# Bias rows, staircase rows and buffers of an attention and MLP kernel moved in its first stage

## The chip, the cores and the metric

One NeuronCore of a Trainium2 chip runs the whole program. The metric is device time in microseconds (us), the median over several executions. The kernel before has a median of 371.52 us in 11 runs (368.65 to 373.35). One further execution was profiled; it took 371.14 us, of which 369.4 us are its span, from the first to the last recorded instruction, and 1.74 us lie around it.

The core has five instruction queues. PE (TensorE) multiplies matrices, ACT (ScalarE) applies functions, DVE (VectorE) works on elements, POOL (GpSimd) does slower element work here and issues DMAs, and SP (SyncE) only issues DMAs. Every queue is worked off in order. PEld in the profile is the load of a stationary operand for PE.

## The reference

Eight batches of eight heads, 576 positions, head size 64, causal attention with an extra bias made of a cumulative sum, then a two-layer MLP whose activation is a hard swish:

```python
scores = scale * np.matmul(q, k.transpose(0, 1, 3, 2))
s_pos = np.maximum(s, 0.0)
cum = np.cumsum(s_pos, axis=-1)
bias = -(cum[:, :, :, None] - cum[:, :, None, :])
scores = np.where(causal, -1000000000.0, scores + np.minimum(bias, 0.0))
...
attn = attn / (np.sum(attn, axis=-1, keepdims=True) + 1e-09)
out = np.matmul(attn, v)
...
h = x @ w_in
g = h * np.clip(h + 3.0, 0.0, 6.0) / 6.0
return (g @ w_out).astype(np.float32)
```

x has 4608 rows (batch times position) and 512 columns (head times head size); w_in is 512 by 2048.

## The kernel before, in words

**Pairs.** The 64 heads are taken two at a time: 32 pairs p, four pairs (PPB) to a batch. The loop over p at L576 does the attention of a pair, and from p = 4 on it weaves in groups of the MLP (`group()`, L478: `m1` is the first layer, `m2` the second), as the batches become complete. The order of instructions on each engine is the order of the program text; no scheduler changes it.

**One q and k tile per pair.** A pair lives in one of NQK = 3 tiles `qks[p % 3]` (L84). Partitions 0 to 63 hold q and k transposed. Partitions 64 to 67 hold four bias rows, so that one matmul over 68 partitions adds the bias; `load_aug` (L135) copies them there out of `aug`, with one DMA for each head of the pair, 9 KB each. Partitions 68 to 127 hold a staircase, a constant pattern that makes masked entries of a diagonal block large and negative when the matmul runs over all 128 partitions. The staircase is used by pairs 4 and up; the first four pairs add a mask with a matmul of their own (`add_mask`, L273) and read 68 partitions only. `set_stair` (L506) writes it, two copies over partitions 64 to 127, so bias rows must be loaded after it. Before the change all three tiles get their staircase before the loop: tile 0 on DVE, tile 1 on ACT, tile 2 on DVE.

**The way of q, k and v.** SP loads q and k of a pair into `raws` (`load_qk`, L106) and v into `vraws` (`load_v`, L122). POOL casts q and k to 16 bits (`cast_qk`, L183) and v (`cast_v`, L198). PE transposes q and k (`transpose`, L217) and ACT and DVE copy the result into `qks`. In the loop, `get(i)` (L594) is the transpose for pair p+1, `scores(p, hh, g)` (L282) one of three parts of the scores of head hh with its exponential on ACT, `corner` (L317) the last 64 positions of both heads, `av` (L343) the product with v, `norm` (L373) the division on DVE. `scores` and `corner` of a pair wait for its bias rows.

**Who issues what.** On SP, after the first loads, the order is: bias rows of pair 0 (L561), q, k of pair 2, v of pair 1, q, k of pair 3, v of pair 2 (L562 to L567); then in iteration p: bias rows of pair p+2 (L579, for p below 4), q and k of pair p+4, v of pair p+3. On POOL: bias rows of pair 1 (L570), casts of v 0, q and k 1, v 1; then in iteration p: bias rows of p+2 (from p = 4), cast of q and k of p+2, cast of v of p+1, and one piece of the MLP weights (`next_weights`, L163: w_in in two pieces, w_out in four), a DMA that also casts to 16 bits.

**Semaphores of SP's DMAs.** SP's and ACT's DMAs go round eight semaphores; a DMA waits until the eighth before it has landed. So SP has at most eight transfers under way.

**Masks.** For pairs 4 and up, DVE takes the minimum of the exponentials and a mask (`masks_sb`, 128x640, L313 and L337).

Of the kernel before, what the change touches and what calls it, by code (L numbers as in the profile page):

```python
# [9 lines left out]
F32 = mybir.dt.float32  # L10
F16 = mybir.dt.float16
# [7 lines left out]
def kernel(  # L19
# [10 lines left out]
    nc = tc.nc  # L30
# [9 lines left out]
    NKC = DM // 128  # L40
    NFT = DFF // 128
    NBLK = NT // 512
    SPAD = 768
    NPE = 2 * PPB + 1
    NQK = 3
    NRAW = 3
    VW = 66

# [2 lines left out]

    jj, ii = np.arange(128)[:, None], np.arange(128)[None, :]
    tri = np.where(jj <= ii, 65504.0, 0.0)
    tri4 = np.where((jj <= ii) & (jj < 64), 65504.0, 0.0)[:, 0:64]
    masks_dram = nc.inline_tensor(
        np.concatenate([tri] * 4 + [tri4] * 2, axis=1).astype(np.float16), name="masks"
    )
    grp = (np.arange(128) * 61 // 128)[None, :]
    steps_r = np.arange(1, 61)[:, None]
    stair = np.zeros((128, 2, 128), np.float32)  # L60
# [13 lines left out]
    def keep(name, shape, dt, n=1):  # L74
        made = [
            cpool.tile(shape, dt, name=f"{name}{i}", tag=f"{name}{i}") for i in range(n)
        ]
        return made if n > 1 else made[0]
# [10 lines left out]
    w_in_sb = keep("w_in_sb", [128, NKC, DFF // 2], F16, 2)  # L89
    w_out_sb = keep("w_out_sb", [128, 4, DM], F16, 4)  # L90
    ident = keep("ident", [128, 128], F16)
    masks = keep("masks_sb", [128, 640], F16)
    neg_sb = keep("neg_sb", [128, 128], F16)
    stair_sb = keep("stair_sb", [128, 2, 128], F16)
    bias3 = keep("bias3", [128, 1], F32)
# [149 lines left out]
    def spread(p, i):  # L245
        jt, qk = J[p], qks[p % NQK]
        for par, n in ((0, 3), (1, 2)):
            c = 9 * i + par
            r, sl = 64 * (c % 2), c // 2
            src = jt[r : r + 64, sl : sl + n, :]  # L250
            ap = [list(x) for x in src.ap]
            ap.insert(1, [256, 2])
            nc.vector.tensor_copy(  # L253
                out=qk[0:64, :, i, 128 * par : 128 * par + 256 * n].rearrange(
                    "p h (s two c) -> p h s two c", two=2, c=128
                )[:, :, :, 0, :],
                in_=bass.AP(src.tensor, src.offset, ap),
            )

# [22 lines left out]
    def scores(p, hh, g):  # L282
        qT, kT = qk_of(p, hh)
        pt = Pof(p, hh)
        S = s_bank([128, 512], "S")
        masked = p < PPB
        if g == 0:
            if masked:
                add_mask(S, 128, 4)
            for j in range(4):  # L290
                c = slice(128 * j, 128 * (j + 1))
                mm(  # L292
                    S[:, c],
                    lhsT=kT[0:68, c] if masked else kT[:, c],
                    rhs=qT[0:68, c] if masked else qT[:, c],
                    start=(j == 0 and not masked),
                    stop=(j == 3),
                )
        else:
            for j in ((0, 3) if g == 1 else (1, 2)):  # L300
                c = OFF[j] - 512 * g
                w = 448 - 128 * j
                mm(  # L303
                    S[:, c : c + w],
                    lhsT=kT[0:68, 128 * j : 128 * (j + 1)],
                    rhs=qT[0:68, 128 * (j + 1) : SEQ],
                    start=(c == 0),
                    stop=(c != 0),
                )
        c = slice(512 * g, 512 * (g + 1))  # L310
        nc.scalar.activation(out=pt[:, c], in_=S, func=AF.Exp, scale=0.125)  # L311
        if g == 0 and not masked:
            nc.vector.tensor_tensor(  # L313
                out=pt[:, c], in0=pt[:, c], in1=masks[:, c], op=ALU.min
            )

    def corner(p):  # L317
        S = s_bank([128, 2, 64], "Sc")
        masked = p < PPB
        if masked:  # L320
            add_mask(S, 64, 2)
        for hh in range(2):
            qT, kT = qk_of(p, hh)
            r = 68 if masked else 128
            mm(  # L325
                S[:, hh, :],
                lhsT=kT[0:r, 512:640],
                rhs=qT[0:r, 512:576],
                start=(hh == 0 and not masked),
                stop=(hh == 1),  # L330
            )
        pc = PCs[p % 2][:, 0:128]
        nc.scalar.activation(
            out=pc, in_=S.rearrange("p h c -> p (h c)"), func=AF.Exp, scale=0.125
        )
        if not masked:
            nc.vector.tensor_tensor(out=pc, in0=pc, in1=masks[:, 512:640], op=ALU.min)  # L337

# [152 lines left out]

    s_all = work.tile([NHEADS, SEQ], F32, tag="s_all", bufs=1)
    nc.sync.dma_start(out=s_all, in_=s.rearrange("b h t -> (b h) t"))
    nc.scalar.dma_start(out=stair_sb, in_=stair_dram.ap())
    nc.scalar.dma_start(out=ident, in_=ident_dram.ap())
    load_qk(0, 0, nc.sync)
    load_qk(0, 1, nc.scalar)
    nc.scalar.dma_start(out=masks, in_=masks_dram.ap())  # L500
    nc.scalar.preload_act_table_set("natural_log_exp_and_others")
    load_v(0, nc.sync)
    for i in range(2):
        load_qk(1, i, nc.sync)

    def set_stair(i, copy):  # L506
        for hh in range(2):
# [8 lines left out]
    fill(nc.gpsimd, aug[:, 1:4, 0, :], 1.0)  # L516
    for i in range(NQK):
        init_va(i, nc.gpsimd)
    ones = work.tile([NHEADS, SEQ], F32, tag="ones", bufs=1)
    nc.vector.memset(ones, 1.0)  # L520
    nc.vector.memset(bias3, 3.0)
    for i in range(NQK):
        for hh in range(2):
            r = SEQ + 64 * hh
            nc.vector.memset(qks[i][0:64, hh, :, r : r + 64], 0.0)
    for t in Ps:
        fill(nc.vector, t[:, 1536:1664], 1.0)
    for t in PCs:
        fill(nc.vector, t[:, 128:192], 1.0)
    set_stair(0, nc.vector.tensor_copy)  # L530
    set_stair(1, nc.scalar.copy)


    idle = psum.tile([128, 512], F32, tag="s", bufs=2, name="idle")
    for i in range(44):
# [7 lines left out]
    )  # L543
    c8 = work.tile([NHEADS, SEQ], F32, tag="c8", bufs=1)
    nc.vector.tensor_tensor_scan(
        out=c8, data0=ones, data1=spos, initial=0.0, op0=ALU.mult, op1=ALU.add
    )
    nc.scalar.mul(out=aug[:, 0, 0, :], in_=c8, mul=-1.0)
    nc.vector.tensor_copy(out=aug[:, 1, 1, :], in_=c8)
# [4 lines left out]
        out=aug[:, 3, 1, :], in0=r1, in1=aug[:, 2, 1, :], op=ALU.subtract  # L554
    )

    nc.vector.tensor_scalar_add(out=neg_sb, in0=masks[:, 0:128], scalar1=-65504.0)

    cast_qk(0, nc.scalar.copy, nc.scalar.copy)
    transpose(0, 0)  # L560
    load_aug(0, nc.sync)  # L561
    for p in (2, 3):  # L562
        for i in range(2):
            load_qk(p, i, nc.sync)
        if p == 2:
            load_v(1, nc.sync)
    load_v(2, nc.sync)  # L567
    transpose(0, 1)
    set_stair(2, nc.vector.tensor_copy)
    load_aug(1, nc.gpsimd)  # L570
    cast_v(0)
    cast_qk(1, nc.gpsimd.tensor_copy, nc.gpsimd.tensor_copy)
    cast_v(1)


    for p in range(NP):  # L576
        nxt = p + 1 < NP
        if p + 2 < NP:
            load_aug(p + 2, nc.sync if p < PPB else nc.gpsimd)  # L579
            cast_qk(p + 2, nc.gpsimd.tensor_copy, nc.gpsimd.tensor_copy)  # L580
            if p + 2 >= NPE:
                crossbar_qk(p + 2)
        if p and nxt:
            cast_v(p + 1)
        next_weights({0: 1, 2: 1, 3: 1, 4: 1, 5: 1, 6: 1}.get(p, 0))
        if p + 3 < NP:
            for m in (p + 3, p + 4):
                late = NPE <= m < NPE + 2
                if 3 < m < NP and late == (m == p + 3):
                    for i in range(2):  # L590
                        load_qk(m, i, nc.sync)
            load_v(p + 3, nc.sync)

        def get(i):  # L594
            if p + 1 < NPE:
                transpose(p + 1, i)
            elif nxt:
                spread(p + 1, i)

        if p < PPB:  # L600
            scores(p, 0, 0)
            scores(p, 0, 1)
            get(0)
            scores(p, 0, 2)
            corner(p)
            if p:
                av(p - 1, 1, 0)
                av(p - 1, 1, 1)
                norm(p - 1, 1)
            scores(p, 1, 0)  # L610
            get(1)
            scores(p, 1, 1)
            av(p, 0, 0)
            scores(p, 1, 2)
            if p:
                transpose_x(p - 1)
            av(p, 0, 1)
            norm(p, 0)
            continue

        if p == PPB:
            av(p - 1, 1, 0)
            av(p - 1, 1, 1)
            norm(p - 1, 1)
            scores(p, 0, 0)
            scores(p, 0, 1)
            transpose_x(p - 1)
            early[0] = False
            scores(p, 0, 2)
            get(0)  # L630
            group()
            group()
        else:
            scores(p, 0, 0)
            get(0)
            group()
            scores(p, 0, 1)
            av(p - 1, 1, 0)
            group()
            scores(p, 0, 2)  # L640
            av(p - 1, 1, 1)
            norm(p - 1, 1)
            group()
        corner(p)
        group()
        if p > NPE:
            x_done[0] = p - 1
        scores(p, 1, 0)
        get(1)
        group()  # L650
        scores(p, 1, 1)
        av(p, 0, 0)
        if p >= NPE:
            crossbar_x(p - 1)
        group()
        scores(p, 1, 2)
        if PPB < p < NPE:
            transpose_x(p - 1)
        group()
        av(p, 0, 1)  # L660
        norm(p, 0)
        group()
# [40 lines left out]
```

## Time and profile before

| what | value |
|---|---|
| median of 11 runs | 371.52 us (368.65 to 373.35) |
| profiled execution | 371.14 us, span 369.4 us |
| mean granted TensorE clock | 0.975 of full speed |
| PE busy, 10.7 to 26.3 us / 26.3 to 29.0 us / 42.2 to 46.5 us | 14.63 of 15.6 us / 0.00 of 2.7 us / 0.04 of 4.3 us |
| PE busy, 120 to 240 us | 120 of 120 us |
| q1 (the queue of SP's DMAs) | 48.26 MB, 66.5% of 16 DMA engines' span |
| q0 (the queue of POOL's DMAs) | 4.70 MB, 6.9% |
| q10 (the queue of ACT's DMAs) | 0.56 MB, 0.6% |

How to read it: an engine that is busy for its whole span sets the time; where the busiest engine stands still, the view of waits says what ended the standstill, and that is what set the time there. A row of a timeline has the start in us from the span's start, the duration, the engine (SPq, POOL and so on), the line of the program, the operation, its output and input tiles, how many instructions were merged, and in brackets the idle time ahead of it with what ended that. A row of windows has the stretch, its length, each engine's busy time, the granted TensorE clock (PEclk, 1.00 is full speed), the share of the DMA engines and the rate in GB/s; the share can pass 1, since transfers of an engine overlap.

### The profile page before, as it was taken

The page shows a single profiled execution, that of the slowest core. Times are in us where ns is not written, and L with a number is a line of the kernel's source. Part 1 is how long each engine was busy: PE and PEld are TensorE (multiplying, and loading weights), DVE is VectorE, ACT ScalarE, POOL GpSimd, SP SyncE. Part 2 cuts the span into 40 slices and gives each one's busy share as a digit, 9 for nine tenths or more (in the row PEclk, how much of TensorE's full clock was granted, in tenths as well). Part 3 has the DMA queues.
Part 4 walks back from the last instruction along what each step waited for, and adds up shares of the span by engine and source line. Part 5 has one row for each costly group of instructions (what it writes and reads, how often), then busy time and mean ns, then how long its engine had stood idle before and what let it go on. Part 6 is the DMA issues. An engine that isn't in the chain of part 4 may idle for free.

```text
span 369.4 us, 7713 instructions
## 1 busy us (share of the span) xinstructions
PE 348.0 (94%) x2897; PEld 203.1 (55%) x2897; DVE 238.1 (64%) x539; ACT 223.2 (60%) x388; POOL 105.4 (29%) x201
## 2 busy tenths in 40 slices
PE   6788597989999999999999999999999999999996
PEld 5566365655556555555555555555555544444442
DVE  7475649787777777777777777777775644544531
ACT  6686567866667666666666666666666344344310
POOL 2656184443335333333333333333200000000000
PEclk9598989999999999999999999999999999999999
DMA  8899999699998999998897999997311010010012
GB/s 204 194 215 170 248 224 227 146 214 206 183 176 171 209 210 179 143 212 178 177 179 158 198 174 146 209 178 137 80 50 48 28 57 30 28 57 31 28 57 87
DMA packets 147774, 54.02 MB, mean 146 GB/s; under 512 B 137520, under 2 KB 141312, under 8 KB 147736
## 3 DMA queue, kind: packets, MB, share of 16 engines
q1 hardware_dynamic: 143736, 48.26, 66.5%
q0 software_dynamic: 3360, 4.70, 6.9%
q10 hardware_dynamic: 640, 0.56, 0.6%
q8 instruction: 23, 0.38, 0.5%
q14 instruction: 15, 0.12, 0.1%
HBM read 37.11 MB, written 9.44 MB: 126 GB/s over the span
## 4 chain that ended last, share of the span: by engine, by line
PE 86%; DMA 5%; ACT 4%; DVE 2%; POOL 1%; issue 1%; ACTq 0%
PE po L442 33%; PE ph L420 32%; PE O L356 7%; PE S L303 7%; DMA qk<-aug 5%; PE S L292 4%; PE pt L221 1%; ACT tr L430 1%; ACT P L311 1%; DVE gT L431 1%; ACT qk L508 1%; DVE x L379 1%; PE Sc L325 1%; PE ptx L393 0%; PE S L274 0%
## 5 line engine op out<-in xcount | busy, mean ns | idle before, releaser
L431 DVE SCALAR_TENSOR_TENSOR gT<-tr,ph 128x512 f16<-128x512 f32 x144 | 98.7, 685 | 91.8 <-ACT tr L430 90.9
L420 PE MATMUL ph<-xT,w_in_sb 128*128 128x512 f16 x576 | 149.1, 381 | 0.0
L442 PE MATMUL po<-w_out_sb,gT 128*128 128x512 f16 x576 | 145.5, 379 | 0.0
L430 ACT ACTIVATE tr<-ph,bias 128x512 f32<-128x512 f32 x144 | 99.0, 688 | 76.0 <-PE ph L420 66.1
L311 ACT ACTIVATE P<-S 128x512 f16<-128x512 f32 x192 | 112.3, 595 | 50.9 <-PE S L292 31.4
L420 PEld LDWEIGHTS <-w_in_sb 128*128 128x128 f16 x576 | 59.0, 114 | 39.1 <-issue 0.8
L442 PEld LDWEIGHTS <-gT 128*128 128x128 f16 x576 | 49.9, 97 | 45.5
L138 POOL DMA_DIRECT2D qk<-aug x54 | 31.4, 582 | 131.8 <-PE Sc L325 59.0
L303 PE MATMUL S<-qk 68*128 68x448 f16 (+3 forms) x256 | 51.3, 283 | 0.7 <-ACT P L311 0.7
L356 PE MATMUL O<-va,P 128*128 128x65 f16 x896 | 49.7, 197 | 1.3 <-DVE x L379 1.0
L356 PEld LDWEIGHTS <-P 128*128 128x128 f16 x896 | 40.9, 100 | 15.2 <-DVE x L379 1.6
L303 PEld LDWEIGHTS <-qk 68*128 68x128 f16 x256 | 24.5, 102 | 23.6 <-issue 1.5
L292 PE MATMUL S<-qk 128*128 128x128 f16 (+1 forms) x256 | 25.7, 225 | 9.2 <-DMA qk<-aug 8.5
L379 DVE TENSOR_TENSOR x<-O,rl 128x320 f16<-128x320 f32 x64 | 31.5, 492 | 2.2
L292 PEld LDWEIGHTS <-qk 128*128 128x128 f16 (+1 forms) x256 | 19.9, 100 | 23.5 <-issue 9.9
L253 DVE COPY qk<-jt 64x768 f16<-64x768 f16 x92 | 29.9, 325 | 1.3
L451 DVE TENSOR_SCALAR ob<-po 128x512 f32<-128x512 f32 x36 | 24.6, 683 | 9.5 <-PE po L442 9.5
L192 POOL CAST tok<-raw 128x576 f16<-128x576 f32 x46 | 29.5, 674 | 3.8 <-DMA raw<-in_k_dram 2.6
L313 DVE TENSOR_TENSOR P<-P,masks_sb 128x512 f16<-128x512 f16 x56 | 24.4, 435 | 9.2 <-ACT P L311 9.1
L200 POOL CAST va<-vraw 128x512 f16<-128x512 f32 x32 | 20.1, 628 | 13.2 <-DMA vraw<-in_v_dram 11.1
L230 DVE COPY qk<-pt 64x576 f16<-64x576 f16 x22 | 16.6, 753 | 7.6 <-PE pt L221 5.2
L188 POOL CAST tok<-raw 96x768 f16<-96x768 f32 x16 | 12.9, 827 | 8.0 <-DMA raw<-in_q_dram 4.9
(44 smaller groups left out, 139.8 us busy)
## 6 DMA issues: line engine op xcount, KB each, us to landing
raw<-in_q_dram SPq DMA_DIRECT2D x32, 288.0 KB, 5.1
out_dram<-ob SPq DMA_DIRECT2D x36, 256.0 KB, 2.0
raw<-in_k_dram SPq DMA_DIRECT2D x31, 288.0 KB, 5.5
vraw<-in_v_dram SPq DMA_DIRECT2D x64, 128.0 KB, 4.4
w_in_sb<-in_moe_w_in_dram POOLq DMA_DIRECT2D x2, 1024.0 KB, 9.5
w_out_sb<-in_moe_w_out_dram POOLq DMA_DIRECT2D x4, 512.0 KB, 7.5
vraw<-in_v_dram SPq DMA_DIRECT2D x32, 32.0 KB, 4.0
qk<-aug POOLq DMA_DIRECT2D x54, 9.0 KB, 3.5
```

The source lines that it names most:

```text
L138: eng.dma_start(out=qks[p % NQK][64:68, hh, :, 64 * hh : 64 * hh + SEQ], in_=aug[g : g + 1, :, :, :],)
L192: eng(out=tok[:, 9 * D * i : 9 * D * (i + 1)], in_=raws[p % NRAW][:, 9 * D * i : 9 * D * (i + 1)],)
L253: nc.vector.tensor_copy(out=qk[0:64, :, i, 128 * par : 128 * par + 256 * n].rearrange("p h (s two c) -> p h s two c", two=2, c=128)[:, :, ...
L292: mm(S[:, c], lhsT=kT[0:68, c] if masked else kT[:, c], rhs=qT[0:68, c] if masked else qT[:, c], start=(j == 0 and not masked), stop=(j == 3),
L303: mm(S[:, c : c + w], lhsT=kT[0:68, 128 * j : 128 * (j + 1)], rhs=qT[0:68, 128 * (j + 1) : SEQ], start=(c == 0), stop=(c != 0),)
L311: nc.scalar.activation(out=pt[:, c], in_=S, func=AF.Exp, scale=0.125)
L356: mm(o[:, i, :], lhsT=lhsT, rhs=va[:, hh, j, 0:65], **kw)
L379: nc.vector.tensor_tensor(out=X[p][:, :, hh, :], in0=o[:, :, 0:64], in1=rl.to_broadcast([128, 5, 64]), op=ALU.mult,)
L420: mm(ph, lhsT=w_in_sb[ft // 8][:, kc, c : c + 512].rearrange("p (u r) -> p r u", r=4)[:, ft % 4], rhs=xT[:, kc, n * 512 : (n + 1) * 512], ...
L430: nc.scalar.activation(out=tr, in_=ph, func=AF.Relu, bias=bias3[:, 0:1])
L431: nc.vector.scalar_tensor_tensor(out=gTs[n][:, ft, :], in0=tr, scalar=6.0, in1=ph, op0=ALU.min, op1=ALU.mult)
L442: mm(po, lhsT=gTs[n][:, ft, t4 * 128 : (t4 + 1) * 128], rhs=w_out_sb[ft // 4][:, ft % 4, :], start=(ft == 0), stop=(ft == NFT - 1),)
```

## The change

- Four q and k tiles (and four of v's tiles `va`) in place of three; a row of the tile is 704 elements wide, not 768.
- `load_aug(0)` to `load_aug(3)` are issued on SP one after the other, ahead of q and k of pair 2. Before, pair 1's were on POOL and those of pairs 2 and 3 on SP in iterations 0 and 1.
- The three `set_stair` ahead of the loop are gone, and the staircase constant is loaded on SP after v of pair 2, not first on ACT's queue. `late_rows(p + 3)` writes the staircase of one tile on DVE and then loads the bias rows of pair p+3 on SP; it stands in iterations 1 to 3 after `get(1)`, and in iteration 4 after `norm(p - 1, 1)`. These are the bias rows of pairs 4 to 7. In SP's queue they come after q and k of pair p+4 and v of pair p+3 of the same iteration. That leaves the rows of pairs 4 and 5 where they were: after v of pair 4, and after v of pair 5. Those of pairs 6 and 7 move from POOL to SP.
- From iteration 5 on, POOL issues the bias rows of pair p+3, not p+2.
- q and k of pair 1 are loaded ahead of v of pair 0 and cast ahead of it.
- The mask constant is one 128x128 triangle, read four times by a broadcast, in place of 128x640. The constant `ones` is one column, broadcast.
- The zero fill of the tiles' ends covers 128 partitions, since the staircase no longer overwrites it early.

```diff
-    SPAD = 768
+    SPAD = 704
-    NQK = 3
+    NQK = 4
...
-    masks = keep("masks_sb", [128, 640], F16)
+    tri_sb = keep("tri_sb", [128, 128], F16)
...
         if g == 0 and not masked:
+            diag = pt[:, c].rearrange("p (j c) -> p j c", j=4)
             nc.vector.tensor_tensor(
-                out=pt[:, c], in0=pt[:, c], in1=masks[:, c], op=ALU.min
+                out=diag,
+                in0=diag,
+                in1=tri_sb[:, None, :].to_broadcast([128, 4, 128]),
+                op=ALU.min,
             )
...
-    nc.scalar.dma_start(out=stair_sb, in_=stair_dram.ap())
     nc.scalar.dma_start(out=ident, in_=ident_dram.ap())
     load_qk(0, 0, nc.sync)
     load_qk(0, 1, nc.scalar)
-    nc.scalar.dma_start(out=masks, in_=masks_dram.ap())
+    nc.scalar.dma_start(out=tri_sb, in_=masks_dram.ap())
     nc.scalar.preload_act_table_set("natural_log_exp_and_others")
-    load_v(0, nc.sync)
     for i in range(2):
         load_qk(1, i, nc.sync)
+    load_v(0, nc.sync)
...
-    ones = work.tile([NHEADS, SEQ], F32, tag="ones", bufs=1)
+    ones = work.tile([NHEADS, 1], F32, tag="ones", bufs=1)
...
-            nc.vector.memset(qks[i][0:64, hh, :, r : r + 64], 0.0)
+            nc.vector.memset(qks[i][:, hh, :, r : r + 64], 0.0)
...
-    set_stair(0, nc.vector.tensor_copy)
-    set_stair(1, nc.scalar.copy)
...
-        out=c8, data0=ones, data1=spos, initial=0.0, op0=ALU.mult, op1=ALU.add
+        out=c8, data0=ones.to_broadcast([NHEADS, SEQ]), data1=spos, initial=0.0, op0=ALU.mult, op1=ALU.add
...
     load_aug(0, nc.sync)
+    load_aug(1, nc.sync)
+    load_aug(2, nc.sync)
+    load_aug(3, nc.sync)
     for p in (2, 3):
         for i in range(2):
             load_qk(p, i, nc.sync)
...
     transpose(0, 1)
-    set_stair(2, nc.vector.tensor_copy)
-    load_aug(1, nc.gpsimd)
+    nc.sync.dma_start(out=stair_sb, in_=stair_dram.ap())
+    cast_qk(1, nc.gpsimd.tensor_copy, nc.gpsimd.tensor_copy)
     cast_v(0)
-    cast_qk(1, nc.gpsimd.tensor_copy, nc.gpsimd.tensor_copy)
     cast_v(1)
+
+    def late_rows(p):
+        set_stair(p % NQK, nc.vector.tensor_copy)
+        load_aug(p, nc.sync)
 
     for p in range(NP):
         nxt = p + 1 < NP
+        if p > PPB and p + 3 < NP:
+            load_aug(p + 3, nc.gpsimd)
         if p + 2 < NP:
-            load_aug(p + 2, nc.sync if p < PPB else nc.gpsimd)
             cast_qk(p + 2, nc.gpsimd.tensor_copy, nc.gpsimd.tensor_copy)
...
             scores(p, 1, 0)
             get(1)
+            if p:
+                late_rows(p + 3)
             scores(p, 1, 1)
...
             norm(p - 1, 1)
+            late_rows(p + 3)
             scores(p, 0, 0)
```

More of the change, by code (lines that the diff above doesn't have):

```diff
@@ L53 @@
     tri = np.where(jj <= ii, 65504.0, 0.0)
[L54 to L57, printed above, removed]
+    masks_dram = nc.inline_tensor(tri.astype(np.float16), name="masks")
     grp = (np.arange(128) * 61 // 128)[None, :]
@@ L252, in spread @@
             ap.insert(1, [256, 2])
+            dst = qk[0:64, :, i, 128 * par : 128 * par + 128]
+            to = [list(x) for x in dst.ap]
+            to.insert(2, [256, n])
             nc.vector.tensor_copy(
-                out=qk[0:64, :, i, 128 * par : 128 * par + 256 * n].rearrange(
-                    "p h (s two c) -> p h s two c", two=2, c=128
-                )[:, :, :, 0, :],
+                out=bass.AP(dst.tensor, dst.offset, to),
                 in_=bass.AP(src.tensor, src.offset, ap),
@@ L331, in corner @@
             )
[L332 to L335, printed above, removed]
+        pc = PCs[p % 2][:, 0:128].rearrange("p (h c) -> p h c", h=2)
+        nc.scalar.activation(out=pc, in_=S, func=AF.Exp, scale=0.125)
         if not masked:
-            nc.vector.tensor_tensor(out=pc, in0=pc, in1=masks[:, 512:640], op=ALU.min)
+            nc.vector.tensor_tensor(
+                out=pc,
+                in0=pc,
+                in1=tri_sb[:, None, 0:64].to_broadcast([128, 2, 64]),
+                op=ALU.min,
+            )
     O, X = {}, {}
@@ L555 @@
     )
-    nc.vector.tensor_scalar_add(out=neg_sb, in0=masks[:, 0:128], scalar1=-65504.0)
+    nc.vector.tensor_scalar_add(out=neg_sb, in0=tri_sb, scalar1=-65504.0)
     cast_qk(0, nc.scalar.copy, nc.scalar.copy)
```

## The prediction

> **What bounds the kernel now.** I read the page's head and slices first, then PE's timeline for the places where it stands still, then the queues of those who end a standstill (SP, POOL, the DMA engines).
>
> ```profile
> span 369.4 us, 7713 instructions
> ...
> PE 348.0 (94%) x2897; PEld 203.1 (55%) x2897; DVE 238.1 (64%) x539; ACT 223.2 (60%) x388; POOL 105.4 (29%) x201
> ...
> PEclk9598989999999999999999999999999999999999
> DMA  8899999699998999998897999997311010010012
> ```
>
> A slice is 9.2 us. PE is busy 94% of the span and after the first five slices it hardly rests; all that can be won early lies in the first 46.5 us. There the DMA engines are full too, and PEclk is low in three places. PE's timeline shows three waits for data:
>
> ```profile
> 17.72 0.52 PEld L221 LDWEIGHTS <-tok 96*128 96x128 f16 x6 [0.22 <-POOL tok L188]
> ...
> 29.01 0.38 PE L292 MATMUL S<-qk 68*128 68x128 f16 x4 [2.71 <-DMA qk<-aug]
> ...
> 46.51 0.38 PE L292 MATMUL S<-qk 128*128 128x128 f16 x4 [4.27 <-DMA qk<-aug]
> ```
>
> The first is iteration 1's transpose of pair 2, just in time; the second is pair 3 waiting for its bias rows, the third pair 5 for its own. From 46.5 us on the waits view has no DMA among PE's releasers: what moves that point moves the end by as much. So the question is what sets 46.5. SP's queue:
>
> ```profile
> 8.53 1.54 SPq L138 DMA_DIRECT2D qk<-aug  x2
> 10.12 0.43 SPq L110 DMA_DIRECT2D raw<-in_q_dram  x1
> ...
> 16.54 1.48 SPq L138 DMA_DIRECT2D qk<-aug  x2
> 18.11 0.38 SPq L110 DMA_DIRECT2D raw<-in_q_dram  x1
> ...
> 20.89 1.74 SPq L138 DMA_DIRECT2D qk<-aug  x2
> ...
> 31.35 1.50 SPq L138 DMA_DIRECT2D qk<-aug  x2
> ...
> 40.90 1.39 SPq L138 DMA_DIRECT2D qk<-aug  x2
> ```
>
> The five rows of bias loads belong to pairs 0, 2, 3, 4 and 5. Issuing one pair's 18 KB takes SP about 1.5 us, as long as three loads of q at 0.4 to 0.5 us and 288 KB each. POOL's queue:
>
> ```profile
> 16.05 0.61 POOL L200 CAST va<-vraw 128x512 f16<-128x512 f32 x1 [2.95 <-DMA vraw<-in_v_dram]
> ...
> 16.85 1.59 POOL L188 CAST tok<-raw 96x768 f16<-96x768 f32 x2
> 18.39 0.78 POOL L144 DMA_DIRECT2D w_in_sb<-in_moe_w_in_dram  x1
> ...
> 30.67 0.61 POOL L200 CAST va<-vraw 128x512 f16<-128x512 f32 x1 [7.40 <-DMA vraw<-in_v_dram]
> ...
> 31.47 0.76 POOL L144 DMA_DIRECT2D w_in_sb<-in_moe_w_in_dram  x1
> ```
>
> POOL waits for v of pair 1 until 16.05, casts pair 2 (PE's 17.72 waits for that) and issues weights; it waits for v of pair 3 until 30.67, and issues the next weights. What weights do to SP's loads is in the DMA queues from 22 to 24 us:
>
> ```profile
> q0 software_dynamic: 183, 0.37, 102.1%
> q1 hardware_dynamic: 74, 0.02, 7.2%
> ```
>
> q0 (POOL's weights) takes all, q1 (SP's loads) next to nothing. In the same view q0 fills 21.5 to 27.3 (first piece of w_in) and 33 to 43 (second piece, first of w_out). So there is one chain without PE: q of pair 2 issued 10.12, v of pair 1 landed 16.05, weights issued 18.39, q0 full until 27.3, v of pair 3 landed 30.67, weights issued 31.47, q0 full until 43, bias rows of pair 5 (behind v of pair 5) landed 46.4. PE's waits are only its slack against this chain.
>
> **The change, part by part.**
>
> *Bias rows at the head of SP's queue.* Three pairs more, six DMAs, come between 8.53 and q of pair 2. One pair costs 1.53 (mean of the five rows) and 0.06 to the next: 3 x 1.59 = 4.8 us. By the cheapest row (1.39) it is 4.4, by the dearest (1.74) 5.4. q of pair 2 is issued at about 14.9 in place of 10.12, and the engines have little else then: their share is 0.62 from 8 to 10 us and 0.37 from 10 to 12 already. Everything behind is late with it: v of pair 1, the cast (17.72 becomes about 22.3), the weights.
>
> *What comes back.* ACT's queue loses 192 KB of constants ahead (its q10 carries 0.56 MB), so s may land earlier: DVE waited 0.41 for it; I take 0.2, between 0 and 0.4. The pairs' rows no longer sit at 16.54 and 20.89. Behind 20.89 the engines were full, nothing is won; behind 16.54 their share dips to 0.71 in 18 to 20 us beside 1.16: 2 x 0.45 / 1.15 = 0.8 us of transfer refilled (ends 0 and 0.8). The staircase (64 KB at some 240 GB/s) costs 0.3 there. Sum for the chain: 4.8 - 0.2 - 0.8 + 0.3 = 4.1; I take 4.0. The dip at 32 to 34 us (share 0.73) follows v of pair 3's landing and shifts with it; if it were filled too, 0.7 less.
>
> *The wait that is removed.* Pair 3's rows now lie ready, so 2.71 us of standstill at 29.01 goes. It pays nothing: iteration 1 starts its transposes 4.6 later, and next late in iteration 3 is v of pair 3 (cast 30.67 + 4 + 0.9). Pairs 4 and 5's rows keep their places in SP's queue, so the 46.51 start becomes about 50.5, and the later standstill of about 4 us stays.
>
> *The clock.* Granted 0.50 in 10 to 18 us and 0.52 in 18 to 20, then 1.00; 0.54 in 30 to 32 and 0.50 in 48 to 50, after the standstills. With 5 us of waiting in iteration 1 (from about 16.9 to 22.3) it should stay at half until about 26. Matmuls of the mask then take 0.61 in place of 0.38; iterations of that stage are held by ACT's exponentials, and I add 0.5 us for each of two. Cover: the wait for v of pair 3 and for pair 5's rows, 4 us; without it, 1 us.
>
> The Trainium skill ("TensorE: Matmul & The Clock Gate", "HAM oscillation — how this bites in real kernels") says that idle gaps over about 3.4 us cost PE half its clock; that speaks against a change that opens a gap of 5 us, and by its 1.67 us of throttled time for each gap it would add less than 1 us, as an estimate. The row of this trace is dearer: 0.54 and 0.61 over 30 to 34 us after only 2.71 us of standstill.
>
> The same skill ("DMA: Bandwidth & Descriptors", "Queues, rings and completion order") says that the engines take turns between queues packet by packet. By that rule SP's loads would get a share beside the weights, and the late weights would matter less; the 102.1% against 7.2% above disagree, and I go by them. By the rule alone the loss would be the queue's shift without the weights', nearer 3 than 4.
>
> *Late staircases and rows of pairs 4 to 7.* 2 x 0.49 on DVE (row of L508) in iterations 1 to 4, ahead of the copy of xT and the norm. DVE is busy 8.80 of 15.6 us (10.7 to 26.3), so it fits; if not, up to 1 us in each of three iterations, and PE waits for O's bank. The first staircase waits for its constant, loaded behind v of pair 2; behind it on SP stand q and k of pair 6. The rows of pairs 6 and 7 cost SP 2 x 1.5 near 47 and 52 us, ahead of q and k of pair 8; pair 9's cast waits for loads at 61.46, but its spread reads at 74.2, so this is covered. Cost of a failed cover: 3 us.
>
> *Costed at nothing.* The staircases ahead of the loop (DVE 0.93 and 0.89, ACT 2.41): ACT's multiply of `aug` could start 0.6 earlier, but SP waits for DVE's chain from s to L553, which has no gap behind 3.92. One more zero fill (0.11 each) and three more of `va` on POOL lie ahead of that. Broadcast masks: nearest rows 0.435 contiguous and 0.75 for 64x576 in 32 bits; by the dearer rate 0.23 more, twice a pair, where DVE is busy 29.48 of 40 us (80 to 120): hidden (uncovered 56 x 0.23 = 13 us; a gain I exclude, nothing is read less than before at that rate). The scan with a broadcast operand: I keep its 1.35; ends 0.75 (the subtract of that shape) and 2.3 (by strided to contiguous copies, 0.76 to 0.45), which would put -0.6 to +0.9 on the chain. POOL saves 1.44 at 9.12; it then waits for v anyway.
>
> **The rivals.**
>
> *Slower (the forecast):* 371.5 + 4.0 = 375.5 (in the profiled execution 369.4 + 4.0 + 1.74 = 375.1, which stood 0.4 under the median). Its own range is 373.5 to 377.2.
>
> *Faster:* v of pair 3 moves ahead of the first weights, which are issued 4.5 later. It decides when its last packet leaves before about 26; then it lands some 3 us before 30.67, iteration 3 has no wait, the weights run on end, and pair 5's rows land about 1.5 earlier, with the half clock after 46.5 (about 1 us) saved: 369. Against it: before, v of pair 3 was issued 19.14, two us before q0 filled, and did not get through; q, k of 4 shift as much as the weights.
>
> *No change:* dips refilled (0.8 and 0.7), s early, and the first piece of w_out falls behind pair 5's rows (some 3 us of q0): 4.8 - 4.7, 371.6. For it: the engines dip three times. Against: w_out is issued by the same chain.
>
> *Slower still:* DVE's staircases and the half clock outlast the cover, or the rows of pair 6 come late behind the third weights: 2 to 3 more, 378.
>
> **How the numbers follow.** Forecast 0.55, slower still 0.10, no change 0.17, faster 0.18. Half a per cent, 1.9 us, is about what a measurement of this kernel tells from no change. The forecast and worse are slower (0.65), the faster case is faster (0.18), the rest is same (0.17). The range goes from 370.3, which takes in no change, to 378.0.
>
> **What would show it.** Right: q of pair 2 issued near 14.9; PE waiting about 5 us ahead of the transposes of pair 2 (near 22); no wait for bias rows in iteration 3; v of pair 3 cast near 34.7; pair 5's scores starting near 50.5 after a wait for bias rows; the same rows after it, 4 us later. Wrong: bias rows issued in well under 1.4 us a pair, v of pair 3 ahead of the weights, or pair 5 starting before 48.

## The result, and the profile after

The changed kernel takes 375.15 us (median of 12 runs, 372.32 to 378.47) beside 370.34 us of the kernel before (47 runs on the same chip, 367.9 to 374.52). The ratio is 1.0119, with a 95% interval from 1.009 to 1.0148: slower, by about 4.4 us. Ratios here leave out executions over 1.5% slower than their kernel's fastest (one of e1 took 604.61 us), so they aren't quite the quotients of the medians. The profiled execution has a span of 373.9 us, 4.5 more than the 369.4 before, and its own time of 375.86 us stands 0.7 above the median.

The head and the slices of the changed kernel's page come first (a slice is 9.35 us):

```profile
span 373.9 us, 7721 instructions
...
PE 349.6 (93%) x2897; PEld 203.9 (55%) x2897; DVE 243.3 (65%) x545; ACT 220.6 (59%) x386; POOL 102.6 (27%) x198
...
PEclk9559689999999999999999999999999999999998
DMA  8299999999989999898997999998411011010012
```

PE has the same 2897 instructions. Its busy time is 1.6 us longer than before (349.6 beside 348.0), at a mean granted clock of 0.961 beside 0.975; the other 2.9 of the 4.5 us are standstill. The second slice of the line DMA is new: it was 8 and is 2. In this slice, from 9.35 to 18.7 us, the DMA engines' share is 0.27, where it was 0.90, and PEclk stays at half speed through the second and the third slice.

SP's queue in the timeline of the changed kernel shows why (start, duration, line, transfer, count; the last two rows are those of pairs 4 and 5):

```profile
9.72 5.50 SPq L135 DMA_DIRECT2D qk<-aug  x8
15.27 0.44 SPq L107 DMA_DIRECT2D raw<-in_q_dram  x1
...
33.03 2.86 SPq L135 DMA_DIRECT2D qk<-aug  x2
...
39.90 2.37 SPq L135 DMA_DIRECT2D qk<-aug  x2
```

For 5.50 us SP issues nothing but bias rows, eight DMAs of 9 KB at 0.69 us each (5.50 / 8), and q of pair 2 leaves at 15.27 instead of 10.12. The windows view has what the DMA engines did meanwhile (time, length, busy time of PE, PEld, DVE, ACT, POOL, then granted clock, DMA share and GB/s), first in the kernel before:

```profile
10.00:14.00 4.00, 2.63 (x19) 1.78 (x20) 1.74 (x4) 1.90 (x4) 3.05 (x5) 0.50 0.73 182
```

and in the changed one:

```profile
10.00:14.00 4.00, 2.64 (x19) 1.74 (x19) 2.25 (x4) 1.48 (x4) 1.10 (x3) 0.51 0.04 10
...
18.00:22.00 4.00, 0.36 (x2) 0.00 (x0) 0.00 (x0) 1.06 (x2) 0.57 (x2) 0.50 1.00 242
```

From 10 to 14 us the engines move 10 GB/s; before it was 182 GB/s in the same four microseconds. The bill is paid from 18 to 22 us, where PE is busy for 0.36 of 4 us and waits for what was issued late. POOL's timeline, which holds the chain behind SP:

```profile
21.43 0.61 POOL L197 CAST va<-vraw 128x512 f16<-128x512 f32 x1 [10.27 <-DMA vraw<-in_v_dram]
22.22 1.59 POOL L185 CAST tok<-raw 96x768 f16<-96x768 f32 x2
23.76 0.90 POOL L141 DMA_DIRECT2D w_in_sb<-in_moe_w_in_dram  x1
...
35.20 0.61 POOL L197 CAST va<-vraw 128x512 f16<-128x512 f32 x1 [5.46 <-DMA vraw<-in_v_dram]
35.99 0.77 POOL L141 DMA_DIRECT2D w_in_sb<-in_moe_w_in_dram  x1
```

v of pair 1 is cast at 21.43 instead of 16.05, the first weights leave at 23.76 instead of 18.39, v of pair 3 is cast at 35.20 instead of 30.67, the second weights leave at 35.99 instead of 31.47. And PE's timeline, at the places where it stands still:

```profile
23.10 0.66 PE L218 MATMUL pt<-ident,tok 96*128 96x96 f16 x6 [4.73 <-POOL tok L185]
...
35.86 0.41 PE L361 MATMUL O<-va,P 128*128 128x65 f16 x8 [1.19 <-POOL va L197]
...
39.55 0.61 PE L290 MATMUL S<-qk 128*128 128x128 f16 x4 [1.42 <-DMA qk<-aug]
...
50.93 0.50 PE L290 MATMUL S<-qk 128*128 128x128 f16 x4 [2.59 <-DMA qk<-aug]
```

The wait of 2.71 us for pair 3's bias rows is gone, as the change means it to be. In its place stand 4.73 us for the transposes of pair 2 and two short ones; pair 5 (last line) starts its scores at 50.93 instead of 46.51, 4.42 us later, and the span is 4.5 longer. Behind it little differs: 322.9 us from there to the end before, 323.0 after.

### The profile page after: what moved, and what is told of

It reads as the page before. It is cut to its first block, busy times and chain, and to the rows that moved or that the text cites. A ratio compares the mean times of both kernels' runs of the same rounds, so it can differ in the third digit from the quotient of the medians.

```text
span 373.9 us, 7721 instructions
## 1 busy us (share of the span) xinstructions
PE 349.6 (93%) x2897; PEld 203.9 (55%) x2897; DVE 243.3 (65%) x545; ACT 220.6 (59%) x386; POOL 102.6 (27%) x198
## 4 chain that ended last, share of the span: by engine, by line
PE 84%; DMA 8%; DVE 3%; SPq 2%; ACT 2%; POOL 1%; issue 1%; POOLq 0%
PE po L447 33%; PE ph L425 32%; PE O L361 7%; PE S L301 6%; DMA qk<-aug 5%; PE S L290 3%; DMA raw<-in_k_dram 2%; SPq L135 1%; DMA vraw<-in_v_dram 1%; ACT tr L435 1%; DVE gT L436 1%; PE pt L218 1%; ACT P L309 1%; DVE x L384 1%; PE ptx L398 1%; SPq L107 1%
## 5 line engine op out<-in xcount | busy, mean ns | idle before, releaser
L135 POOL DMA_DIRECT2D qk<-aug x48 | 27.7, 577 | 119.3 <-PE Sc L327 57.5
L312 DVE TENSOR_TENSOR P<-P,tri_sb 128x512 f16<-128x512 f16 x56 | 25.3, 452 | 7.2 <-ACT P L309 7.0
L218 PE MATMUL pt<-ident,tok 96*128 96x96 f16 x108 | 9.1, 231 | 6.8 <-POOL tok L185 4.7
```

Of the source, the lines that this page charges most:

```text
L135: eng.dma_start(out=qks[p % NQK][64:68, hh, :, 64 * hh : 64 * hh + SEQ], in_=aug[g : g + 1, :, :, :],)
```

## The experiments

Twelve runs follow, of eleven kernels (g3 is f4 once more). All ratios are to the kernel before, measured beside them on the same chip. All compute the whole reference.

| run | median us | ratio | 95% interval |
|---|---|---|---|
| the change | 375.15 | 1.0119 | 1.009 to 1.0148 |
| e1, rows of pairs 1 to 3 on POOL | 370.47 | 1.001 | 0.9971 to 1.0048 |
| e2, pair 1 behind v of pair 0 | 373.95 | 1.007 | 1.0037 to 1.0104 |
| e4, staircases early | 375.1 | 1.011 | 1.0048 to 1.0171 |
| e6, four more row DMAs | 377.44 | 1.0157 | 1.0106 to 1.0208 |
| f1, before, weights late | 368.28 | 0.9953 | 0.9919 to 0.9988 |
| f2, e1 and rows of pairs 4 to 7 on POOL | 368.97 | 0.9966 | 0.9934 to 0.9999 |
| f3, f2 and weights late | 368.25 | 0.9962 | 0.9926 to 0.9998 |
| f4, the change, weights late | 374.44 | 1.0112 | 1.0071 to 1.0154 |
| g1, two pairs' rows behind v of pair 1 | 374.24 | 1.0102 | 1.0067 to 1.0138 |
| g2, g1 and weights late | 373.22 | 1.0074 | 1.0039 to 1.011 |
| g3, f4 again | 372.99 | 1.0068 | 1.003 to 1.0106 |
| g4, two pairs' rows on POOL | 371.56 | 1.0013 | 0.9985 to 1.004 |

### e1: the rows of pairs 1 to 3 from POOL's queue

```diff
     load_aug(0, nc.sync)
-    load_aug(1, nc.sync)
-    load_aug(2, nc.sync)
-    load_aug(3, nc.sync)
...
     cast_v(0)
+    for p in (1, 2, 3):
+        load_aug(p, nc.gpsimd)
     cast_v(1)
```

> Theory (the chain SP's bias rows -> v of pair 1 -> weights -> rows of pair 5 sets the time, PE only waits for it): the six DMAs of pairs 1 to 3 leave SP's queue, where eight took 5.50 us. q of pair 2 is issued near 11.2 in place of 15.27, v of pair 1 cast near 17.3 in place of 21.43, pair 5's scores start near 46.8 in place of 50.93: 4 us less than the changed kernel, about equal to before (ratio 1.000, 0.996 to 1.004). Rival (the late staircases on DVE, the half clock and the broadcast masks cost the time): all of these stay, so the ratio stays near 1.012.

Measured: 1.001 (0.9971 to 1.0048). Three lines of its timeline, one each of SP, POOL and PE, in order of time:

```profile
10.61 0.43 SPq L107 DMA_DIRECT2D raw<-in_q_dram  x1
...
11.13 3.53 POOL L135 DMA_DIRECT2D qk<-aug  x6
...
44.56 0.38 PE L290 MATMUL S<-qk 128*128 128x128 f16 x4 [1.96 <-DMA qk<-aug]
```

The same six DMAs cost POOL 3.53 us while it would wait for v anyway; q of pair 2 leaves SP at 10.61, and pair 5 starts at 44.56. Everything else of the change is still in this kernel: late staircases, broadcast masks, pair 1's early loads, the broadcast operand of the scan. Its interval and that of the change don't touch, so the loss belongs to those six DMAs in SP's queue, and the other edits together cost nothing that can be measured (the interval allows half a per cent either way).

### e2: pair 1's q and k behind v of pair 0 again

```diff
+    load_v(0, nc.sync)
     for i in range(2):
         load_qk(1, i, nc.sync)
-    load_v(0, nc.sync)
...
+    cast_v(0)
     cast_qk(1, nc.gpsimd.tensor_copy, nc.gpsimd.tensor_copy)
-    cast_v(0)
     cast_v(1)
```

> q and k of pair 1 go behind v of pair 0 again, in the loads and the casts. Theory: the rows' start moves from 9.72 back to about 8.6, since s lands 0.5 earlier and DVE's last subtract (1.39) no longer runs beside POOL's cast (0.75 before): the chain and the end move 1.1 earlier, ratio 1.009. Rival (the early cast of pair 1 helps): iteration 0 waits 1 us for its transposes again and the ratio rises to 1.014.

Measured: 1.007 (1.0037 to 1.0104), an interval that overlaps that of the change. The expected gain didn't come: the rows start at 9.70 here, 9.72 in the change. DVE's first step on s starts at 4.79 (4.47 in the change), so the place of pair 1's loads isn't what makes s late; and DVE's last subtract takes 1.04 us, again beside casts on POOL, now those of v of pair 0. The order of pair 1 and v has no cost or gain that this run can tell.

### e4: the staircases early again

```diff
+    nc.scalar.dma_start(out=stair_sb, in_=stair_dram.ap())
     nc.scalar.dma_start(out=ident, in_=ident_dram.ap())
...
-    nc.sync.dma_start(out=stair_sb, in_=stair_dram.ap())
...
+    set_stair(0, nc.vector.tensor_copy)
+    set_stair(1, nc.scalar.copy)
+    set_stair(2, nc.vector.tensor_copy)
+    set_stair(3, nc.scalar.copy)
...
     def late_rows(p):
-        set_stair(p % NQK, nc.vector.tensor_copy)
         load_aug(p, nc.sync)
```

> The four staircases are written ahead of the loop again (two on DVE, two on ACT) and their constant is loaded first on ACT's queue; the rows of pairs 4 to 7 stay where they are. Theory: PE's waits are slack, so what DVE saves in iterations 1 to 4 pays nothing; SP saves one issue of 0.6, and ACT's two copies (1.25 each) may delay the chain's start: within 1 us of the changed kernel, ratio 1.010 to 1.014. Rival (late staircases on DVE are the cost): 2 to 4 us faster, ratio 1.001 to 1.007.

Measured: 1.011 (1.0048 to 1.0171), an interval that reaches into the rival's range, so this time alone doesn't decide. e1 does: it has the late staircases and no loss, so they aren't the cause. The trace of e4 holds a lesson beside it. Here v of pair 3 gets through ahead of the first weights (its cast begins at 28.03 and the second weights leave at 29.76; 35.20 and 35.99 in the change), which is the condition of the prediction's faster rival. It doesn't pay, as this line of PE's timeline of e4 shows:

```profile
42.73 0.61 PE L290 MATMUL S<-qk 128*128 128x128 f16 x4 [5.91 <-DMA qk<-aug]
```

Pair 4's bias rows now stand behind the weights, and PE waits 5.91 us for them; pair 5 starts at 50.76, in the change at 50.93. In this execution, what is won at one place of the queue is lost at the next.

### e6: four more row DMAs at the head of SP's queue

```diff
     load_aug(3, nc.sync)
+    load_aug(3, nc.sync)
+    load_aug(3, nc.sync)
```

> The rows of pair 3 are loaded three times over at the head of SP's queue: four DMAs more. Theory: 4 x 0.69 = 2.75 us more for everything behind, so pair 5's scores start near 53.7 and the ratio becomes 1.019. Rival (SP's queue has slack behind PE's wait of 2.59 at pair 5): ratio stays 1.012.

Measured: 1.0157 (1.0106 to 1.0208). The interval holds both expectations, so the time decides nothing. The trace (SP's and PE's timeline) follows the theory at the near end only:

```profile
9.12 9.45 SPq L135 DMA_DIRECT2D qk<-aug  x12
...
26.15 0.66 PE L218 MATMUL pt<-ident,tok 96*128 96x96 f16 x6 [8.86 <-POOL tok L185]
```

Four more DMAs take 3.95 us more of SP (9.45 less 5.50). In 1.1 us of this SP waits for earlier rows to land, as its waits view says; the rest is 0.7 for each. PE's wait for the transposes of pair 2 grows from 4.73 to 8.86, by 4.13. At the far end the theory failed: v of pair 3 is cast at 31.87, 3.3 us sooner than in the change, and pair 5's scores start at 51.40 without a wait, only 0.47 later than there and not at 53.7. By the ratios, the time grows by 0.4% (1.4 us), and the two intervals overlap. So in this execution most of the later start was made up farther on.

### f1 and f4: the weights of iteration 3 moved to iteration 6

f1 is the kernel before with this edit, f4 the changed one.

```diff
-        next_weights({0: 1, 2: 1, 3: 1, 4: 1, 5: 1, 6: 1}.get(p, 0))
+        next_weights({0: 1, 2: 1, 4: 1, 5: 1, 6: 2}.get(p, 0))
```

> The kernel before, with one thing moved: the first piece of w_out is issued in iteration 4, not 3, the second in 5 and the last two in 6. Theory (the weights' queue shuts SP's loads out while it runs): the stretch of some 4 us in which q0 carries this piece no longer stands ahead of pair 5's rows, so they land near 43 in place of 46.4, PE comes there at 42.2, and the half clock behind the standstill (1 us) goes too: 3 to 4 us less, ratio 0.990. Rival (the queues take turns, SP's loads are limited by themselves): ratio 0.998 to 1.000.

> The changed kernel with the weights moved as in the first. Theory: pair 5's scores start near 47.5 in place of 50.93, ratio 1.002 to 1.004. Rival (the loss is SP's own queue alone): 1.012 stays.

f1 measured 0.9953 (0.9919 to 0.9988): faster than before by about 2 us, half of what was expected, and the interval also holds the rival's 0.998. In its trace pair 5 starts 3.1 us sooner than before and hardly waits (PE's timeline):

```profile
43.38 0.38 PE L292 MATMUL S<-qk 128*128 128x128 f16 x4 [0.67 <-DMA qk<-aug]
```

So in the kernel before the weights that POOL sends in iteration 3 do hold up pair 5's rows. f4 measured 1.0112 (1.0071 to 1.0154): the same edit gave the changed kernel nothing, which the rival had expected. Its profiled execution differs (span 369.7, pair 5 at 46.25), but it was among the fastest of its ten, 371.65 us where the median is 374.44.

### g3: f4 once more

> The kernel of f4 once more, for its profile: the first one's execution (369.7 us of span, pair 5 at 46.25) was among the fastest of its ten, which went from 371.3 to 377.0 us. Theory: the others lose their 3 to 5 us at the rows of pair 5 or 6 behind weights, so an execution of 372 us or more of span shows pair 5 at 48 or later. Rival: pair 5 starts near 46 in it too and the time is lost behind 57 us, at DVE. Ratio 1.011 (1.006 to 1.015) again.

Measured: 1.0068 (1.003 to 1.0106), an interval that overlaps the one of f4. In this execution (span 371.6) PE has no wait at pair 5, which starts at 48.66, after a start that was late by itself: the rows' issue began at 10.71, in f4 at 8.83. Between these two points pass 37.95 us here and 37.42 in f4. Both statements are only half right: pair 5 is beyond 48, as the theory said, but not because of weights; and 1.58 us are lost in one wait for DVE's xT at 79.36, behind 57 us, where the rival had put the loss. By the two runs of this kernel together, late weights bring the changed kernel somewhere between 0 and 2 us; most of its loss is not in the weights' queue.

### f2 and f3: all early rows on POOL, then the weights late too

f2 is e1 with this edit; f3 is f2 with the edit of f1.

```diff
     def late_rows(p):
         set_stair(p % NQK, nc.vector.tensor_copy)
-        load_aug(p, nc.sync)
...
+        if 2 <= p <= PPB + 1:
+            load_aug(p + 2, nc.gpsimd)
         if p > PPB and p + 3 < NP:
             load_aug(p + 3, nc.gpsimd)
```

> From the kernel with the rows of pairs 1 to 3 on POOL: the rows of pairs 4 to 7 go to POOL's queue too, one iteration after their staircase; SP issues only pair 0's. Theory: pair 5's rows no longer stand behind v of pair 5 and what shuts it out; its wait (1.96 at 44.56 in that kernel) goes, and next late are k of pair 6 and v of pair 5, a little earlier: 1 to 2 us less than that kernel, ratio 0.995 to 0.998. Rival (on POOL's queue the rows stand behind the weights themselves): no gain, 1.001 or worse.

> The kernel before this one, with the weights moved as in the first: if both theories hold, the gains add up to some 4 to 6 us and PE stands still less than 1 us from iteration 2 to 8, ratio 0.985 to 0.990. If the pieces of w_out become late for the second layer, PE waits for them near 65 to 80 us and the ratio is 0.995 or more.

f2 measured 0.9966 (0.9934 to 0.9999), as expected, though its interval overlaps e1's, so a gain over e1 isn't shown. f3 measured 0.9962 (0.9926 to 0.9998): the two gains do not add. Neither trace has a wait for pair 5's rows left (its scores start at 43.43 in f2 and 44.21 in f3), so the second edit finds nothing to remove. In f3 PE still waits, 1.48 us at 34.75 and 1.21 at 37.53, but for DVE's x and not for pieces of w_out. f1, f2 and f3 beat both kernels; the kernel before is beaten by 1.4 to 2.1 us, each time with an interval below 1 (in f2 and f3 just below). Which of the three is best can't be told.

### g1 and g4: the same place in the queue, another number of DMAs

Both keep only the rows of pair 1 ahead of q of pair 2. Those of pairs 2 and 3 are issued by SP behind v of pair 1 in g1, and by POOL in g4.

```diff
     load_aug(0, nc.sync)
     load_aug(1, nc.sync)
-    load_aug(2, nc.sync)
-    load_aug(3, nc.sync)
...
         if p == 2:
             load_v(1, nc.sync)
+            load_aug(2, nc.sync)
+            load_aug(3, nc.sync)
```

and g4, in place of the two lines added in g1:

```diff
     cast_v(0)
+    for p in (2, 3):
+        load_aug(p, nc.gpsimd)
     cast_v(1)
```

> The changed kernel with the bias rows of pair 1 ahead of q and k of pair 2 on SP, but those of pairs 2 and 3 only behind v of pair 1; the number of issues is the same. Theory (what costs is the place, not the number): q of pair 2 is issued 4 x 0.69 = 2.8 us earlier than in the changed kernel (near 11.6 to 12.5), PE waits some 2 us instead of 4.7 for the transposes of pair 2, and pair 5 starts near 48: ratio 1.003 (0.999 to 1.007). Rival (SP's queue as a whole decides, so the number counts): the rows push v of pair 2 and everything behind it back by the same 2.8 us, and the ratio stays at 1.010 to 1.013.

> As g1, but the bias rows of pairs 2 and 3 are issued by POOL, behind the cast of v of pair 0, and not by SP behind v of pair 1: those of pair 1 alone stand ahead of q of pair 2, and SP issues four DMAs fewer in all. The place of q of pair 2 is that of g1 (2.9 us behind the start of the rows). Theory (SP's queue as a whole decides, so the number of its early issues counts): of the 4.8 us of the change two thirds come back, ratio 1.004 (1.000 to 1.008). Rival (only what stands ahead of q of pair 2 counts): the same as g1, 1.010 (1.007 to 1.014).

g1 measured 1.0102 (1.0067 to 1.0138), g4 1.0013 (0.9985 to 1.004); the intervals lie apart. SP's timeline, first of g1:

```profile
9.51 2.85 SPq L135 DMA_DIRECT2D qk<-aug  x4
12.40 0.44 SPq L107 DMA_DIRECT2D raw<-in_q_dram  x1
...
15.16 2.66 SPq L135 DMA_DIRECT2D qk<-aug  x4
17.94 0.37 SPq L107 DMA_DIRECT2D raw<-in_q_dram  x1
```

and of g4:

```profile
9.82 2.85 SPq L135 DMA_DIRECT2D qk<-aug  x4
12.71 0.44 SPq L107 DMA_DIRECT2D raw<-in_q_dram  x1
...
15.55 0.52 SPq L107 DMA_DIRECT2D raw<-in_q_dram  x1
```

In both, q of pair 2 leaves 2.89 us after the first row. They part behind it: q of pair 3 leaves at 17.94 in g1, behind four more row DMAs, and at 15.55 in g4. That difference makes 0.9% of the time. So the DMAs that stand ahead of the loads behind q of pair 2 count too, not only those ahead of q of pair 2: g1's theory fell, and the same thought as g4's theory held. That it is their number alone isn't shown. The kernel before issues six such DMAs early on SP, more than g4's four, and doesn't pay; there two pairs' rows stand behind v of pair 2 and v of pair 3, so place and number weren't tried apart. What stays open is where g1 loses its time: its profiled execution, with pair 5 at 48.01 as g1's theory had it, is the shortest of its ten (372.6 us beside a median of 374.24) and doesn't show the loss.

### g2: g1 with the weights late

> g1 with the weights' piece of iteration 3 moved to iteration 6. If the two causes add, PE waits some 2 us for the transposes of pair 2 and hardly at all for the rows of pair 5, which starts near 44.5: ratio 0.995 (0.991 to 1.000). Rival (what f4 showed: with the rows on SP the later weights give nothing in most executions): no better than g1, 1.000 to 1.007.

The edits are those of g1 and f1. Measured: 1.0074 (1.0039 to 1.011). The two causes do not add; this is at the upper edge of what the rival gave. In its trace pair 5 starts at 46.01, after a wait of 2.31 us for its rows that the late weights were to remove, and 2.38 us are lost behind that, at 76 us, in a wait for DVE.

## Why the prediction was right

The forecast was 375.5 us and slower; 375.15 was measured. The cost that it names, six more DMAs at the head of SP's queue, is shown: e1 has everything else and measures 1.001. That the number came so close is in part luck: the kernel before stood at 370.34 and not 371.5, the rise was 4.4 us and not 4.0, and the terms erred in both directions. By its steps:

- **What bounds the kernel: seen in these two executions, shown only in part.** The chain without PE moved as a whole in them. The shifts are 5.15 (q of pair 2 issued), 5.38 (v of pair 1 cast), 5.37 (weights), 4.53 (v of pair 3 cast), 4.52 (second weights), 4.42 (pair 5) and 4.5 (the span). From pair 5's start to the end pass 322.9 and 323.0 us, so here it carries the end; in the other runs it is 321.5 to 325.9. Up to the first weights the chain repeats: from q of pair 2 issued to v of pair 1 cast pass 5.93 us before, 6.16 in the change, 5.76 and 5.97 in f4 and g3. The next link doesn't repeat. f4 and g3 have the change's code up to the weights of iteration 3, and v of pair 3 is cast there at 30.27 and 29.64, not 35.20: 21.4 and 18.9 us behind the first bias row, against 25.5 in the change and 22.1 before. So whether the first weights hold up v of pair 3 differs between executions of the same code, and by which link the loss reaches the end of most executions is open.
- **The rows at the head of SP's queue: right, mis-sized.** Six more DMAs were put at 4.8 us and took 3.96 (5.50 less 1.54). A row of two DMAs that stands alone takes about 1.5; eight in one go take 0.69 each.
- **s earlier by 0.2: wrong.** In the changed kernel's execution the rows start 1.19 us later than before (9.72, not 8.53), for two reasons. s is late by itself: DVE's first step on it starts at 4.47 instead of 3.92. In the eleven runs with the changed loads in which DVE waits for s, this step starts between 4.18 and 5.60, and at 3.92 and 3.85 in the two with the code of before (before and f1); the cause is open. And DVE's last subtract of the split takes 1.39 instead of 0.75 us, since casts on POOL now run at that time (the lines are in the last section). Before, POOL stood at the bias rows of pair 1 until 9.12 and cast nothing; the change took them off its queue. The prediction had no term for this. From DVE's first step on s to the rows pass 4.6 us in the runs without this collision and 4.9 to 5.3 in those with it.
- **What comes back (0.8 less 0.3): about right.** Between the first weights and v of pair 3 the shift falls from 5.37 to 4.53, by 0.84; 0.5 had been written. Since this link differs so much between executions of the same code, the agreement says little. The start came out 1.4 dearer than written, the rows 0.8 and the refill 0.3 cheaper; in the profiled executions the sum is 4.5 instead of 4.0. The terms were less well known than the total: errors of 1.4 one way and 1.1 the other cancelled.
- **The removed wait pays nothing: right.** The wait at 29.01 is gone, and the standstill at pair 2 has taken its place. e1 has that wait gone too, without most of that standstill (1.37 us are left), and is no faster than the kernel before.
- **The clock: seen, no separate price.** In the windows from 12 to 26 us the granted clock reads 0.50, as the prediction said. Some of the 1.6 us more of PE's busy time may be its price; no run separates it.
- **Late staircases, masks, scan: right at nothing.** e1 holds them all and is 1.001, within half a per cent. The mask's minimum takes 452 ns with the broadcast operand and 435 without.
- **Where the step was too narrow.** The prediction gave the whole price to q of pair 2 leaving late. g1 and g4 show that the queue behind it counts as well: giving q of pair 2 back 2.66 us (2.89 instead of 5.55 behind the first row) returned nothing that could be measured; taking four DMAs out of SP's queue as well returned nearly all.

Of the rivals, the faster one had its condition met in e4's execution (v of pair 3 ahead of the weights), without its gain. No change is what e1 and g4 give, for another reason than the rival's: with the rows off SP's queue.

## What to carry to other kernels

Here SP's queue, which feeds the whole pipeline, had a price for each DMA that it issued, and not by its size: eight transfers of 9 KB held SP for 5.50 us, while one of 288 KB takes it 0.44. Before small transfers are moved to the front of such a queue, count them, multiply, and look for an engine that only waits at that time; on POOL (e1) the same transfers cost nothing that could be measured. An engine's queue that loses such transfers may also start its next work sooner and get in another's way, as POOL's casts did with DVE's subtract. And read several executions before a time is put down to a place: the medians of g1 and f4 lay 1.6 and 2.8 us above the execution that was profiled.

## What the runs showed of the hardware

The cost of issuing was not small beside the transfer. The Trainium skill ("DMA: Bandwidth & Descriptors", "Issuing engines are not separate DMA queues") says that several issuing engines save only sequencer time, which it calls usually small relative to the DMA itself. For rows of 9 KB the measurement says otherwise: 0.69 us each on SP (0.59 on POOL, 3.53 for six), with the engines' share at 0.04 meanwhile, and 1.1% of the kernel's time between e1 and the change.

DVE's copies slow down beside POOL's casts. DVE's timeline of the changed kernel:

```profile
32.49 0.90 DVE L512 COPY qk<-stair_sb 64x1280 f16<-64x1280 f16 x2
...
36.72 2.40 DVE L512 COPY qk<-stair_sb 64x1280 f16<-64x1280 f16 x2
```

The same two copies take 0.90 us at 32.49, where POOL stands still, and 2.40 at 36.72, where POOL casts q and k from 36.76 to 38.36. The Trainium skill ("SBUF — State Buffer", "Who interferes with whom") says that copies in DVE's two-port modes and GpSimd's instructions exclude each other for a whole instruction. The trace agrees: 0.90 and the casts' 1.60 are 2.50, against the 2.40 measured.

The same slowing meets DVE's last subtract of the split, which the bias rows wait for. Before, in DVE's timeline:

```profile
7.62 0.75 DVE L553 TENSOR_TENSOR aug<-r,aug 64x576 f16<-64x576 f32 x1
```

and in the change, in DVE's and POOL's:

```profile
8.18 1.39 DVE L554 TENSOR_TENSOR aug<-r,aug 64x576 f16<-64x576 f32 x1
...
8.14 0.82 POOL L185 CAST tok<-raw 96x768 f16<-96x768 f32 x1 [4.83 <-DMA raw<-in_q_dram]
```

In the seven of the fourteen profiled executions in which a cast on POOL began before this subtract, the subtract took 1.04 to 1.40 us; in the seven in which none had, it took 0.75.
